# Batch 5 joins the batches whose q is transposed by DMA; the transposing transfers are issued by SyncE, in a new order of work

## The chip, the cores and the metric

The kernel runs on one core of one Trainium2 chip. The metric is device time in microseconds (us) of one execution, inputs and output in HBM. Five engines of the core work side by side, each through its own list of instructions in order: TensorE (PE; its weight loads are shown as PEld), VectorE (DVE), ScalarE (ACT), GpSimd (POOL) and SyncE (SP). Engines wait for each other by semaphores. DMA transfers are issued here by POOL (loads that turn float32 into bfloat16), by SP and by ACT.

## The reference

A linear attention without softmax, normed per head, followed by a gated feed-forward with a convolution over three positions:

```python
batch, n_heads, seq, head_dim = (8, 8, 576, 64)
kv = np.einsum('bhsd,bhse->bhde', k, v)
out = np.einsum('bhsd,bhde->bhse', q, kv)
rms = np.sqrt(np.mean(out * out, axis=-1, keepdims=True) + 1e-06)
attn = (out / rms * g_norm).astype(np.float32)
x = attn.transpose(0, 2, 1, 3).reshape(8, 576, 512)
h = np.maximum(x @ w_in, 0.0)                    # 512 -> 1024
conv_out = sum of conv_w[k] * (h shifted by k - 1 along the sequence), k = 0, 1, 2
gate = 1.0 / (1.0 + np.exp(-conv_out))
result = (h * gate) @ w_out                      # 1024 -> 512
```

The last four lines are shortened; all else is as in the reference.

## The kernel before

**Tiles.** A batch's q, k and v lie in SBUF as 96 partitions by 8 heads by 6 rows of 64 (sequence position = 6 x partition + row), in bfloat16. Two heads make one tile `t` of 128 rows (4 tiles a batch); two tiles make a half `u`. Two batches make a pair `p`.

**Steps**, by their names in the order; the numbers after a name are batch (or pair, or convolution stage), then tile:
- `Lq`, `Lk`, `Lv` (L296), `Li` (w_in), `Lo` (w_out): loads, issued by POOL. q, k and v have two buffers each, so a load waits until the batch two before has been read.
- `kv` (L353): 48 products of 64x64 that sum k^T v over a batch's rows into one PSUM bank; `kvc` copies them into `kvbd`, 128x128 blocks with two heads on the diagonal, zero elsewhere.
- `qt` (L375): TensorE transposes half a batch's q, 24 products; `qc` copies the result to SBUF (`qT`) on DVE or ACT.
- `ot` (L414, L415): q times kvbd for one tile, 64 and then 512 columns at full 128x128.
- For the batches in `QD` (6 and 7) another way: `dq` (L420) issues a transposing DMA of half a batch's q from SBUF to SBUF, which leaves the rows in a different arrangement; `kvn` copies the sums of k^T v without zeros; `kx` (L432), twice, issues a small DMA that puts the other half's rows into `kvx`; `oq` (L442) computes a tile as four 64x64 products of 288 columns at four positions of the array. `sq` and `oc` read that product in the other arrangement.
- `sq` squares the product on ACT, `oc` copies it to SBUF as float32, `ss` sums squares per head on TensorE, `ln` and `sl` make the inverse root, `sp` (L577) spreads it over the rows, `mu` (L584) multiplies into x. Batches 0 and 1 have a shorter way (`on`, `nl`, `mu0`).
- `hm` (L595): x times w_in for one batch and one of 8 blocks `f` of 128 features, 8 products of 288 columns; `re` (L601 on ACT, L603 on DVE) is the relu.
- `ta`, `aa`, `ab` (DVE) make the convolution, `sg` (L656, ACT) the sigmoid, `mg` (DVE) multiplies.
- `om` (L672): h times w_out for 128 rows, 8 products of 512 columns (pairs 0 and 3 in two halves of 4); `ea` copies to one of 8 row buffers; `st` (L683) stores it, issued by SP.
- `unread.n`: n products whose result nobody reads.

**Order.** `ORDER` is one list, written out. The loop at L685 emits one step after the other, and at the end every instruction is tied to its predecessor on its own engine (L695 to L703). So each engine works through its own instructions in the list's order; between engines only data, PSUM banks (the numbers after `@`) and buffers make anyone wait. A step further down the list can start earlier than one above it if it is on another engine. `:1` switches a copy or relu to the other one of ACT and DVE.

What an engine issues counts in this: a `dq` in ACT's list holds back ACT's later steps until it is issued, and a wait in SP's list holds back all later `kx`, `st` and `dq` on SP. In the old order SP issues two loads at the start and then nothing until `kx.6.0`.

Of the kernel before, what the change touches and what calls it, by code (L numbers as in the profile page):

```python
# [73 lines left out]
unread.3@7 ot.1.3@6 sq.1.3@6 ot.1.2@0 aa.0.3 unread.2@2 on.1.3@4 sq.1.2@7 on.1.2@2 ab.0.3 nl.1.3@6 hm.0.3@4 nl.1.2@7
hm.0.2@2 mu0.1.3 mu0.1.2 sg.0.1 sg.0.0 re.0.2:1 Lk.2.0@0 sg.0.6 re.0.3 hm.1.3@0 hm.1.0@6 hm.0.5@2 mg.0.0 hm.0.4@4
ta.0.2@0 sg.0.7 re.1.3 ta.0.3 re.0.5 re.0.4 mg.0.3 aa.0.1 re.1.0 kv.2.0.4@0 hm.1.2@4 kvc.2.0.4.0@0 ab.0.1 ta.0.4@1
sg.0.2 Lq.2.0@0 sg.0.3 ta.0.5 hm.1.7@6 hm.1.6@2 aa.0.2 re.1.2 qt.2.0@4 mg.0.1 ab.0.2 re.1.7 Lq.3.0@1 kvc.2.0.4.1
re.1.6 qt.2.1@0 sg.0.5 sg.0.4 qc.2.0@4 ot.2.1@4 Lv.3.0@1 Lk.3.0@1 sq.2.1@0 ot.2.0@2 sq.2.0@1 qc.2.1@0 ta.1.2@0
hm.1.4@6 ta.1.3 mg.0.2 oc.2.0@0 hm.1.1@0 aa.1.1 re.1.4 oc.2.1 ta.1.0@1 ab.1.1 re.1.1 ot.2.2@2 qt.3.1@6 qt.3.0@4
qc.3.1@1 qc.3.0@2 sq.2.2@2 sg.1.2 sg.1.3 hm.1.5@0 oc.2.2:1@1 ta.1.1 ot.2.3@6 mg.1.1 Lo.0 re.1.5 sq.2.3@3 kv.3.0.4@4  # L80
kvc.3.0.4.0@1 al.x2@1 ss.2@5 al.x1@0 kvc.3.0.4.1 oc.2.3 unread.1@0 ot.3.0@2 sq.3.0@4 oc.3.0@2 Lo.1 ot.3.1@0 aa.1.0
ot.3.2@6 Lq.4.0@0 sq.3.2@5 om.0.3.0@4 ta.1.4@0 ab.1.0 ta.1.5 sq.3.1@6 ln.8@0 om.0.0.0@2 om.0.2.0@3 oc.3.2:1@3 aa.1.2
ot.3.3@6 sq.3.3@7 om.0.0.4 om.0.3.4 om.0.2.4 oc.3.1 oc.3.3 ab.1.2 ea.0.3@0 Lk.4.0@0 sl.8@0 sp.2.0@6,0 ss.3@5
om.0.1.0@4 mu.2.0.0 mu.2.0.1 Lv.4.0@0 ea.0.2@1 ea.0.0@2 ln.1@0 sp.2.1@2,6 mu.2.1.1 mu.2.1.0 om.0.1.4 sg.1.5 sl.1@0
qt.4.1@0 qt.4.0@6 qc.4.1:1@3 ea.0.1@3 hm.2.6@2 hm.2.2@0 qc.4.0@4 re.2.6 sp.3.1@2,6 sg.1.1 re.2.2 kv.4.0.4@4 mu.3.1.0
mu.3.1.1 sg.1.0 mg.1.0 hm.2.4@0 Lv.5.0@1 Lk.5.0@1 kvc.4.0.4.0@0 sp.3.0@6,2 mu.3.0.0 mu.3.0.1 kvc.4.0.4.1 hm.2.5@4
ta.1.6@1 re.2.4 sg.1.4 re.2.5 Lq.5.0@1 ot.4.2@6 hm.2.7@0 ot.4.0@4 sq.4.2@0 Lv.6.0@0 Lq.6.0@0 ta.1.7 oc.4.2@1
Lk.7.0@0 mg.1.2 aa.1.3 sq.4.0@1 hm.3.4@2 re.2.7 re.3.4 hm.3.6@6 ot.4.3@0 ab.1.3 oc.4.0@0 re.3.6 hm.3.5@2 ta.2.4@0
# [25 lines left out]
om.3.7.4 om.2.6.0@4 om.3.5.0@6 om.3.8.0@1 ea.3.3@0 ea.3.0@5 ea.3.7@1 st.3.3 st.1.5 om.3.5.4 om.3.8.4 ea.2.6@0 st.2.5
om.3.2.0@0 om.3.4.0@7 ea.3.5@4 st.2.2 ea.3.8@6 st.3.7 st.3.5 st.3.8 st.3.0 om.3.2.4 om.3.4.4 om.3.6.0@1 om.3.1.0@6
om.3.6.4 ea.3.2@7 st.3.2 st.2.6 om.3.1.4 ea.3.4@1 ea.3.6@4 st.3.4 st.2.1 st.2.0 st.3.6 ea.3.1@6 st.3.1
"""


# [1 line left out]
def kernel(  # L121
# [295 lines left out]
    @op  # L417
    def dq(b, u):
        s = T["qx", b, u] = ring("qT", [P, 2, S], BF16, name="qT").rearrange("p t (h n) -> p (t h n)", n=PS)
        nc.scalar.dma_start_transpose(  # L420
            out=s.rearrange("p (c n) -> p c n", n=PS),
            in_=qkv["q", b][:, 4 * u:4 * u + 4, :].rearrange("p h d -> p (h d)"))

# [310 lines left out]
```

## Time and profile before

| | us |
|---|---|
| median of 3 executions | 182.5 (181.41 to 183.57) |
| the profiled execution, whole | 182.38 |
| its span, first to last instruction | 180.6 |
| PE busy | 170.6 (94% of the span) |
| ACT busy | 149.0 (83%) |
| DVE busy | 140.5 (78%) |
| POOL busy | 31.0 (17%) |
| transposing transfers (4), issue to landing | 4.9 to 5.6, median 5.2 |
| copies into kvx (4), issue to landing | 2.5 to 4.3, median 4.0 |

The granted clock of TensorE is 1.0 throughout. The chain of work that ended last is on PE for 57% of the span and on ACT for 19%. The costliest groups are `hm` on PE (512 products, 67.7 us), `om` on PE (288 products, 65.7 us), the sigmoid (41.8 us) and the relu (39.7 us) on ACT.

In a line of the timeline the first number is the start in us from the span's start, the second how long it took, then engine, source line, operation, output and input tile, and how many instructions were merged. `ACTq` and `SPq` are the sequencers of ACT and SP while they issue a DMA. A bracket gives how long the engine sat idle before the instruction and what, by the profile, it waited for. The ends of products on PE are modelled, so their bars overlap by a little.

### The profile page before, as it was taken

What the parts mean: (1) busy time and instruction counts of PE and PEld (TensorE: products, weight loads), DVE (VectorE), ACT (ScalarE), POOL (GpSimd) and SP (SyncE); (2) the same over time, 40 slices, a digit from 0 to 9 for tenths busy, and PEclk for the clock granted to TensorE, in tenths of its full rate; (3) what the DMA queues carried; (4) which work ended last, traced back from release to release, by engine and by line L of the source; (5) the groups of instructions that cost most, each with busy time, mean ns of one, the idle gap of its engine ahead of it and who ended that gap; (6) DMA issues with size and microseconds to landing.
All of it is one profiled execution on the core that took longest, in us unless ns stands there. A gap on an engine that the chain in (4) does not pass through costs nothing.

```text
span 180.6 us, 4135 instructions
## 1 busy us (share of the span) xinstructions
PE 170.6 (94%) x1700; PEld 100.9 (56%) x1700; DVE 140.5 (78%) x237; ACT 149.0 (83%) x233; POOL 31.0 (17%) x54
## 2 busy tenths in 40 slices
...
GB/s 150 187 183 193 200 201 203 203 205 208 203 204 203 203 204 203 205 207 165 243 237 195 5 0 104 12 4 58 0 331 21 0 0 81 210 3 205 147 279 241
DMA packets 32474, 27.57 MB, mean 153 GB/s; under 512 B 6064, under 2 KB 27848, under 8 KB 32456
## 3 DMA queue, kind: packets, MB, share of 16 engines
...
q8 instruction: 13, 0.21, 0.5%
...
## 4 chain that ended last, share of the span: by engine, by line
PE 57%; ACT 19%; DVE 8%; DMA 5%; POOL 5%; issue 4%; ACTq 1%; POOLq 0%; DVEq 0%
PE bank L672 31%; PE bank L595 21%; ACT h L601 6%; DMA v_sb<-in_v_dram 5%; ACT taps L656 4%; ACT sq L469 3%; ACT L208 2%; ACT o L336 2%; DVE xT L584 2%; POOL q_sb L236 1%; DVE qT L338 1%; PE bank L375 1%; DVE taps L637 1%; DVE taps L638 1%; POOL k_sb L236 1%
## 5 line engine op out<-in xcount | busy, mean ns | idle before, releaser
L595 PE MATMUL bank<-xT,w_in_sb 128*128 128x288 bf16 x512 | 67.7, 286 | 1.1 <-ACT h L601 0.8
L672 PE MATMUL bank<-w_out_sb,h 128*128 128x512 bf16 x288 | 65.7, 379 | 0.0
L595 PEld LDWEIGHTS <-w_in_sb 128*128 128x128 bf16 x512 | 49.1, 98 | 17.0 <-issue 2.5
L672 PEld LDWEIGHTS <-h 128*128 128x128 bf16 x288 | 27.4, 98 | 31.5 <-issue 0.7
L656 ACT ACTIVATE taps<-taps,cwn 128x1152 bf16<-128x1152 bf16 (+1 forms) x40 | 41.8, 1083 | 2.5 <-DVE taps L650 1.6
L601 ACT ACTIVATE h<-bank 128x576 bf16<-128x576 f32 x63 | 39.7, 670 | 4.3 <-DVE taps L638 1.6
L336 ACT ACTIVATE row<-bank 128x512 f32<-128x512 f32 x35 | 20.6, 617 | 11.6 <-PE bank L672 11.1
L662 DVE TENSOR_TENSOR h<-h,taps 128x2304 bf16<-128x2304 bf16 (+1 forms) x20 | 22.2, 1112 | 3.4 <-ACT taps L656 3.4
L644 DVE TENSOR_TENSOR taps<-taps 128x2304 bf16<-128x2304 bf16 (+1 forms) x20 | 22.3, 1115 | 0.3
L650 DVE TENSOR_TENSOR taps<-taps,h 128x2304 bf16<-128x2304 bf16 (+1 forms) x20 | 22.2, 1112 | 0.2
L637 DVE TENSOR_SCALAR taps<-h,cwn 128x1152 bf16<-128x1152 bf16 (+1 forms) x40 | 18.4, 460 | 5.0 <-ACT h L601 5.0
L584 DVE SCALAR_TENSOR_TENSOR xT<-o,cw,bank 128x576 bf16<-128x576 f32 x24 | 18.6, 809 | 2.2 <-PE bank L577 2.1
L469 ACT ACTIVATE sq<-bank 128x576 bf16<-128x576 f32 x28 | 18.4, 694 | 1.0 <-PE bank L415 1.0
L638 DVE TENSOR_SCALAR taps<-h,cwn 128x1152 bf16<-128x1152 bf16 (+1 forms) x40 | 18.0, 451 | 0.0
L336 ACT ACTIVATE o<-bank 128x576 f32<-128x576 f32 x22 | 15.1, 717 | 0.0
L411 PE MATMUL bank<-fill 128*128 128x512 bf16 x35 | 10.8, 435 | 2.5 <-DVE fill L223 1.5
...
L353 PEld LDWEIGHTS <-k_sb 96*64 96x64 bf16 x384 | 7.4, 112 | 3.7 <-issue 3.3
L296 POOL DMA_DIRECT2D v_sb<-in_v_dram x8 | 6.1, 768 | 18.1 <-PE bank L353 17.0
L353 PE MATMUL bank<-v_sb,k_sb 96*64 96x64 bf16 x384 | 8.3, 197 | 0.7 <-DMA v_sb<-in_v_dram 0.3
L375 PEld LDWEIGHTS <-q_sb 96*64 96x64 bf16 x288 | 6.9, 110 | 3.5 <-DMA q_sb<-in_q_dram 1.9
L375 PE MATMUL bank<-ident,q_sb 96*64 96x96 bf16 x288 | 8.1, 208 | 0.7 <-DMA q_sb<-in_q_dram 0.6
...
## 6 DMA issues: line engine op xcount, KB each, us to landing
...
```

Source lines behind the costliest of these rows:

```text
L336: nc.scalar.activation(to, fr, AX.Copy)
L469: nc.scalar.activation(in_order(b, s), product(b, t), AX.Square)
L584: nc.vector.scalar_tensor_tensor(x_tile(b)[:, 2 * u:2 * u + 2, n], T["o32", b, u][:, :, n], g_sb, T["sp", b, e][u][:, :, :HS], op0=AL.mult ...
L595: nc.tensor.matmul(ps[:, e, :HS], w_in_sb[:, t, f * P:(f + 1) * P], x[:, t, e * HS:(e + 1) * HS], start=(t == 0), stop=(t == NT - 1))
L601: nc.scalar.activation(to, fr, AX.Relu)
L637: nc.vector.tensor_scalar_mul(tap[:, 0, f % 2, :n, 8:8 + S], h[:, f], cwn[:, 0, f:f + 1])
L638: nc.vector.tensor_scalar_mul(tap[:, 1, f % 2, :n, :S], h[:, f], cwn[:, 2, f:f + 1])
L644: nc.vector.tensor_add(tap[:, 1, :, :n, :S], tap[:, 0, :, :n, 7:7 + S], tap[:, 1, :, :n, 1:1 + S])
L650: nc.vector.tensor_add(y, y, h[:, 2 * j:2 * j + 2])
L656: nc.scalar.activation(y, y, AX.Sigmoid, scale=cwn[:, 1, f:f + 1])
L662: nc.vector.tensor_mul(h, h, T["tap", c, j][:, 1, :, :n, :S])
L672: nc.tensor.matmul(T["om", p, m], h[:, f, m * P:(m + 1) * P], w_out_sb[:, f, :], start=(f == 0), stop=(f == NF - 1))
```

## The change

Batch 5 is added to `QD`. Its two `qt`, two `qc`, two `kvc` and four `ot` go; two `dq`, one `kvn`, two `kx` and four `oq` come. Every `dq`, those of batches 6 and 7 too, is issued by SP instead of ACT. All steps are put into a new order with new banks and some copies on the other engine. SP's list now runs `dq.5.0 kx.5.0 dq.5.1 kx.5.1 st.0.2 dq.7.0 kx.7.0 kx.6.0 kx.7.1 st.0.3 st.0.1 dq.7.1 dq.6.0 st.0.0 dq.6.1 kx.6.1` and then stores. Loads of batch 5 are now issued as q, v, k (before: v, k, q); those of batches 6 and 7 as k6, v7, k7, q7, v6, q6 (before: v6, q6, k7, k6, v7, q7).

```diff
 SPLIT = (0, 3)
-QD = (6, 7)
+QD = (5, 6, 7)
...
-kv.0.3.1@4,5 kvc.0.3.1.0 on.0.2@2 kvc.0.3.1.1:1 ot.0.3@4 nl.0.2@2 al.h1@0 sqh.0.3.0@3 unread.3@7 onh.0.3.0@2
-qt.1.0@6 sqh.0.3.1 nlh.0.3.0@3 qc.1.0:1@2 onh.0.3.1 unread.3@6 kv.1.0.2@6 mu0.0.2 muh.0.3.0 nlh.0.3.1 Lk.1.2 Lq.1.2
-Lv.1.2 kvc.1.0.2.0@1 kvc.1.0.2.1 muh.0.3.1 al.h0@1 Li.1 Li.2 Lv.2.0@0 unread.3@0 ot.1.1@6 hm.0.0@4 pl sq.1.1@4
...
-sq.4.3@2 ot.4.1@6 kv.5.0.4@4 re.3.5 Lk.6.0@1 oc.4.3 ta.2.5 sq.4.1@3 qt.5.1@2 qt.5.0@0 kvc.5.0.4.0:1@1 qc.5.1@0
-oc.4.1 Lv.7.0@1 ss.4@5 sg.1.6 sg.1.7 hm.3.7@6 kvc.5.0.4.1:1 ot.5.2@2 om.0.4.0@4 qc.5.0@2 ot.5.0@0 re.3.7 sq.5.2@4
-aa.2.2 oc.5.2@2 hm.3.2@6 mg.1.3 Lq.7.0@1 sq.5.0@5 oc.5.0@3 ot.5.3@2 ab.2.2 sq.5.3@6 re.3.2 oc.5.3 sg.2.5 sg.2.4
-om.0.4.4 om.0.5.0@0 ot.5.1@6 om.0.6.0@1 hm.2.0@2 ta.2.6@1 om.0.5.4 sq.5.1@7 om.0.6.4 ta.2.7 ea.0.4:1@4 oc.5.1
-hm.2.3@6 ss.5 ea.0.5@5 aa.2.3 mg.2.2 ab.2.3 ln.2@0 kv.6.0.4@0 hm.3.3@4 ta.2.2@0 ea.0.6@6 dq.6.0@1 re.2.3 re.2.0
-sl.2@0 re.3.3 kvn.6:1 om.0.7.0@1 sp.4.0@6,2 om.0.7.4 mu.4.0.0 mu.4.0.1 sp.5.0@4,6 sg.2.6 kv.7.0.4@0 mu.5.0.0
-mu.5.0.1 hm.2.1@2 sp.5.1@4,6 kx.6.0 st.0.2 ta.2.3 kvn.7 dq.7.0@3 st.0.3 mu.5.1.0 aa.2.1 re.2.1 mu.5.1.1 om.0.8.0@0
-st.0.4 hm.3.1@2 kx.6.1 st.0.1 st.0.5 om.0.8.4 sg.2.7 ea.0.7@7 ab.2.1 hm.3.0@4 dq.6.1@4 re.3.1 sp.4.1@2,6 ea.0.8@1
-al.h2@1 re.3.0 dq.7.1@0 hm.5.3@0 mu.4.1.0 hm.5.1@4 sg.2.3 mg.2.3 re.5.3 mu.4.1.1 ta.2.0@1 ta.2.1 hm.5.2@2 hm.4.1@0
-oq.6.0@6 re.5.1 aa.2.0 ab.2.0 hm.5.7@4 sg.2.2 st.0.8 kx.7.0 al.x3@0 re.4.1 sq.6.0@0 re.5.2 hm.4.2@0 mg.2.1 hm.5.0@2
...
-kx.7.1 re.4.4 oc.6.2@2 oc.6.1 om.1.7.0@6 ea.1.7@0 oq.6.3@2 oq.7.0@4 sq.6.3@3 sq.7.0@4 oq.7.2@0 oc.6.3 oc.7.0@0
...
+unread.3@3 onh.0.3.0@6 nlh.0.3.0@3 onh.0.3.1 qt.1.0@2 nlh.0.3.1 qc.1.0:1@2 mu0.0.2 muh.0.3.0 Lq.1.2 muh.0.3.1 Lv.1.2
+hm.0.6@6 hm.0.7@4 Lk.1.2 re.0.6 re.0.7 unread.3@0 kv.1.0.2@4 kvc.1.0.2.0@1 kvc.1.0.2.1 unread.3@0 ot.1.1@4 ot.1.0@6
+sq.1.1@4 unread.2@0 on.1.1@2 sq.1.0@5 nl.1.1@4 hm.0.0@0 ta.0.6@0 Li.2 re.0.0 ta.0.7 qt.1.1@2 aa.0.3 qc.1.1:1@3
+mu0.1.1 on.1.0@4 Li.1 hm.0.1@0 nl.1.0@5 ta.0.0@1 ab.0.3 kv.1.2.2@2 kvc.1.2.2.0 kvc.1.2.2.1 re.0.1 unread.3@3
+ot.1.2@2 mu0.1.0 ta.0.1 sq.1.2@6 aa.0.0 ot.1.3@6 unread.2@4 on.1.2@0 ab.0.0 sq.1.3@7 nl.1.2@6 Lk.2.0@0 on.1.3@4 pl
...
+kvc.3.0.4.1:1 qt.3.1@2 qc.3.0@1 qc.3.1@2 oc.2.3 Lo.1 Lv.4.0@0 sg.1.3 sg.1.2 Lk.4.0@0 Lq.4.0@0 unread.1@4 ot.3.0@0
+aa.1.2 ot.3.1@6 ot.3.3@2 unread.1@4 om.0.0.0@4 sq.3.0@4 oc.3.0@2 mg.1.1 om.0.1.0@0 sq.3.1@5 Lq.5.0@1 oc.3.1 ot.3.2@6
...
+hm.3.5@6 ot.4.2@2 sq.4.0@0 oc.4.0@0 re.3.5 sq.4.2@1 dq.5.0@0 Lk.6.0@0 hm.3.1@4 hm.2.6@0 ot.4.1@6 mg.1.0 ab.1.3
+ta.2.4@1 re.3.1 oc.4.2@1 sq.4.1@2 ta.2.5 hm.3.3@4 kv.5.0.4@2 oc.4.1 re.2.6:1 aa.2.2 kvn.5:1 sg.1.6 ot.4.3@6 hm.3.6@0
+re.3.3 hm.3.7@4 kx.5.0 sg.1.7 ab.2.2 sq.4.3@3 re.3.6 oc.4.3 hm.2.3@2 hm.3.0@6 hm.2.2@0 mg.1.3 re.3.7 dq.5.1@1
+ta.2.6@0 hm.3.2@4 sg.2.4 re.2.3 kx.5.1 re.3.0 ta.2.7 st.0.2 aa.2.3 re.2.2:1 sg.2.5 oq.5.1@6 oq.5.0@2 re.3.2 sq.5.0@4
+sq.5.1@5 ab.2.3 om.0.8.0@0 hm.2.1@4 oc.5.0@2 re.2.1 Lv.7.0@0 Lk.7.0@1 oc.5.1 om.0.8.4 oq.5.2@2 oq.5.3@4 mg.2.2
+ta.2.2@1 ss.4@1 sq.5.3@6 ta.2.3 sq.5.2@7 om.0.6.0@6 om.0.4.0@7 ss.5 om.0.4.4 ln.2@0 aa.2.1 oc.5.2@3 om.0.6.4
+ea.0.4@4 sl.2@0 ea.0.8@5 kv.7.0.4@7 ea.0.6@6 sp.4.1@0,2 oc.5.3 kvn.7 ab.2.1 mu.4.1.1 mu.4.1.0 om.0.7.0@6 Lq.7.0@0
+Lv.6.0@1 om.0.5.0@7 sp.4.0@2,4 sg.2.2 dq.7.0@2 kx.7.0 Lq.6.0@1 mu.4.0.0 mu.4.0.1 om.0.5.4 sp.5.0@0,2 mu.5.0.0
+mu.5.0.1 om.0.7.4 ea.0.5@7 sg.2.3 kv.6.0.4@7 sp.5.1@0,4 ea.0.7@2 al.x3@0 al.h2@0 hm.4.0@2 kvn.6 mg.2.1 mu.5.1.0
+mu.5.1.1 hm.4.3@6 ta.2.0@1 hm.4.2@0 ta.2.1 sg.2.6 hm.4.4@4 sg.2.7 re.4.3 re.4.0 kx.6.0 kx.7.1 mg.2.3 aa.2.0 re.4.2
+oq.7.0@2 oq.7.1@6 re.4.4 st.0.3 st.0.1 dq.7.1@3 hm.5.2@0 hm.5.3@4 sq.7.0@0 oc.7.0@0 ab.2.0 re.5.2 sq.7.1@1 oc.7.1
+re.5.3 hm.5.0@2 hm.5.5@0 re.5.0 ta.3.2@0 hm.5.4@4 hm.4.1@2 sg.2.0 re.5.5 hm.5.1@0 dq.6.0@4 st.0.0 hm.5.6@6 ta.3.3
+aa.3.1 dq.6.1@0 ab.3.1 sg.2.1 re.4.1 re.5.4 re.5.1 hm.4.6@2 kx.6.1 hm.4.5@0 re.5.6 mg.2.0 ta.3.0@1 om.1.6.0@6 sg.3.2
...
     @op
     def dq(b, u):
         s = T["qx", b, u] = ring("qT", [P, 2, S], BF16, name="qT").rearrange("p t (h n) -> p (t h n)", n=PS)
-        nc.scalar.dma_start_transpose(
+        nc.sync.dma_start_transpose(
             out=s.rearrange("p (c n) -> p c n", n=PS),
             in_=qkv["q", b][:, 4 * u:4 * u + 4, :].rearrange("p h d -> p (h d)"))
```

More of the change, by code (lines that the diff above doesn't have):

```diff
@@ L74 @@
[L74 to L88, printed above, removed]
@@ L114 @@
[L114 to L116 removed]
+pre@0,0,0 unread.10@0 qt0.0.0@0 qc0.0.0:1@0 pn ps pi Lq.1.0@1 ca.k.0 ca.v.0 kv.0.0.1@1 ct@2 qt0.0.1@3 qc0.0.1:1
+kvc.0.0.1.0:1@0 pg kvc.0.0.1.1:1 ot.0.0@0 sq.0.0@0 Li.3 pc al.h0@0 al.x0@0 unread.3@4 kv.0.1.1@3 al.x2@1 Lv.1.0@1
@@ new lines @@
+kvc.0.1.1.0:1 on.0.0@4 nl.0.0@0 Lk.1.0@1 kvc.0.1.1.1:1 al.h1@1 unread.1@6 qt0.0.2@3 ot.0.1@6 sq.0.1@1 unread.4@2
+kv.0.2.1@2 qc0.0.2:1@1 on.0.1@4 mu0.0.0 kvc.0.2.1.0 nl.0.1@1 kvc.0.2.1.1:1 mu0.0.1 qt0.0.3@3 ot.0.2@0 unread.3@2
+kv.0.3.1@2,4 Li.0 sq.0.2@2 qc0.0.3:1 kvc.0.3.1.1 on.0.2@6 kvc.0.3.1.0:1 nl.0.2@2 ot.0.3@4 sqh.0.3.0@3 sqh.0.3.1
+unread.3@3 onh.0.3.0@6 nlh.0.3.0@3 onh.0.3.1 qt.1.0@2 nlh.0.3.1 qc.1.0:1@2 mu0.0.2 muh.0.3.0 Lq.1.2 muh.0.3.1 Lv.1.2
+hm.0.6@6 hm.0.7@4 Lk.1.2 re.0.6 re.0.7 unread.3@0 kv.1.0.2@4 kvc.1.0.2.0@1 kvc.1.0.2.1 unread.3@0 ot.1.1@4 ot.1.0@6
@@ new lines @@
+re.1.4 ta.0.5 kv.2.0.4@0 re.1.6 qt.2.0@6 ab.0.1 qt.2.1@2 aa.0.2 re.1.2 Lv.3.0@1 Lk.3.0@1 sg.0.2 kvc.2.0.4.0:1@0
+sg.0.3 hm.1.3@4 ab.0.2 kvc.2.0.4.1 qc.2.0@4 qc.2.1@0 ot.2.1@6 ot.2.0@0 hm.1.5@2 sg.0.5 sg.0.4 mg.0.1 Lq.3.0@1 re.1.3
+sq.2.0@0 sq.2.1@1 mg.0.2 re.1.5:1 hm.1.7@4 ta.1.2@1 ta.1.3 oc.2.0@0 oc.2.1 ta.1.4@0 ot.2.2@2 re.1.7 hm.1.1@0
+ot.2.3@6 sq.2.2@2 re.1.1 sq.2.3@3 aa.1.1 ta.1.5 Lo.0 ab.1.1 kv.3.0.4@4 kvc.3.0.4.0@1 ss.2@5 oc.2.2@1 qt.3.0@0
+kvc.3.0.4.1:1 qt.3.1@2 qc.3.0@1 qc.3.1@2 oc.2.3 Lo.1 Lv.4.0@0 sg.1.3 sg.1.2 Lk.4.0@0 Lq.4.0@0 unread.1@4 ot.3.0@0
@@ new lines @@
+aa.1.2 ot.3.1@6 ot.3.3@2 unread.1@4 om.0.0.0@4 sq.3.0@4 oc.3.0@2 mg.1.1 om.0.1.0@0 sq.3.1@5 Lq.5.0@1 oc.3.1 ot.3.2@6
+ab.1.2 om.0.2.0@1 ln.8@0 om.0.1.4 sq.3.2@6 sq.3.3@7 oc.3.2@3 om.0.2.4 om.0.0.4 ta.1.0@1 ta.1.1 aa.1.0 sl.8@0 oc.3.3
+ea.0.1@0 sp.2.0@6,2 ss.3@5 al.x1@0 ab.1.0 ea.0.0@1 mu.2.0.1 ln.1@0 mu.2.0.0 om.0.3.0@0 sg.1.5 sp.2.1@4,2 mu.2.1.0
+mu.2.1.1 sl.1@0 om.0.3.4 Lv.5.0@1 sg.1.4 ea.0.2@2 hm.2.7@4 mg.1.2 ta.1.6@0 hm.2.0@2 re.2.7 re.2.0 hm.2.4@6
+sp.3.1@2,4 ea.0.3@3 Lk.5.0@1 kv.4.0.4@1 mu.3.1.0 mu.3.1.1 re.2.4 hm.2.5@6 sg.1.1 sp.3.0@2,4 kvc.4.0.4.0@0 ta.1.7
@@ new lines @@
+ea.1.6@3 st.1.6 ta.3.5 hm.4.7@2 sq.6.2@3 sq.6.0@4 om.1.3.0@6 oc.6.0@2 oc.6.2@3 re.4.7 ea.1.1@0 oq.6.1@0 oq.7.3@2
+aa.3.2 sq.6.1@5 oq.6.3@4 om.1.7.0@7 st.0.5 st.0.7 sq.6.3@6 oc.6.1 sq.7.3@7 ss.6@0 ss.7 om.1.0.0@1 ln.3@0 oc.6.3
+ab.3.2 ea.1.7@1 st.1.1 oc.7.3 om.1.5.0@0 ea.1.0@3 sg.3.4 sl.3@0 sp.7.1@2,4 mu.7.1.1 sg.3.5 om.1.4.0@1 st.1.0
+ea.1.3@7 mu.7.1.0 ea.1.5@2 sp.7.0@2,4 om.1.2.0@7 mu.7.0.0 mu.7.0.1 sp.6.1@4,2 mg.3.2 om.1.8.0@6 mu.6.1.1 st.1.3
+mu.6.1.0 al.h3@1 ta.3.6@0 sg.3.0 hm.5.7@2 ea.1.2@0 ea.1.4@3 ea.1.8@7 sp.6.0@6,4 re.5.7 mu.6.0.0 ta.3.7 mu.6.0.1
```

34 lines of the change are left out of this document (14 added, 20 removed).

## The prediction

> **What bounds the kernel now.** I began with the busy table by stretches. The stretches were cut where the chain of waits changes character: loads and short stages up to 29.4 us, then four stretches up to 177 us, where the last product of w_out ends.
>
> ```profile
> core 0: us, PE busy (x) PEld busy (x) DVE busy (x) ACT busy (x) POOL busy (x), PEclk, DMA share, GB/s
> 29.40:50.00 20.60, 19.81 (x314) 14.73 (x314) 19.44 (x39) 20.48 (x36) 4.72 (x7) 1.00 1.30 204
> 50.00:82.40 32.40, 32.37 (x401) 19.90 (x399) 30.00 (x50) 32.29 (x53) 5.03 (x7) 1.00 1.31 204
> 82.40:98.30 15.90, 15.04 (x200) 9.60 (x196) 15.01 (x25) 12.85 (x19) 0.00 (x0) 1.00 1.14 224
> 98.30:127.00 28.70, 28.69 (x214) 15.63 (x214) 24.79 (x33) 28.64 (x45) 0.00 (x0) 1.00 0.08 29
> 127.00:177.00 50.00, 49.94 (x296) 28.05 (x292) 33.69 (x41) 35.41 (x50) 0.00 (x0) 1.00 0.33 122
> ```
>
> The second number of a line is the stretch, the third PE's busy time. From 29.4 us to 177 us TensorE is idle for 147.6 - 145.85 = 1.75 us only, so a microsecond of TensorE work removed there, or of wait added, counts nearly in full. ACT and DVE are almost as full up to 82 us, so they may take over. The stretch 82.4 to 98.3 is the exception: ACT is busy for 12.85 of 15.9 us. Bars of products overlap and hide short gaps, so I checked it by pace. Eight `hm` groups of 8 products (128 products took 15.79 us in the chain of waits, so 0.99 us a group), four half groups of `om` (144 products in 31.09 us, 0.86 us a half), two `kv` (0.88 us) and four `sp` (0.21 us) make 14.0 us of work in 15.85 us. About 1.9 us is lost, 0.83 us of it in one visible piece. The timeline says why:
>
> ```profile
> 87.99 2.14 ACTq L420 DMA_TRANSPOSE qT<-q_sb  x1
> 88.22 0.36 ACT L336 ACTIVATE kvn<-bank 128x256 bf16<-128x256 f32 x1
> ...
> 89.10 0.52 DVE L638 TENSOR_SCALAR taps<-h,cwn 128x1152 bf16<-128x1152 bf16 x1
> ...
> 90.23 0.65 ACT L601 ACTIVATE h<-bank 128x576 bf16<-128x576 f32 x1 [1.65 <-DVE taps L638]
> ...
> 90.93 1.14 PE L595 MATMUL bank<-xT,w_in_sb 128*128 128x288 bf16 x8 [0.83 <-ACT h L601]
> ```
>
> ACT's sequencer is in the transposing transfer until 90.13 us. The relu behind it starts at 90.23 us, although what the profile names (DVE, L638) ended at 89.62 us; TensorE waits for that relu.
>
> **What leaves TensorE.** The transposes of batch 5 (`qt.5.1`, `qt.5.0`) and the products of one batch before and after, from the timeline of PE:
>
> ```profile
> 57.85 1.21 PE L375 MATMUL bank<-ident,q_sb 96*64 96x96 bf16 x48
> 58.99 2.13 PE L595 MATMUL bank<-xT,w_in_sb 128*128 128x288 bf16 x16
> ...
> 109.89 0.31 PE L442 MATMUL bank<-qT,kvn 64*64 64x288 bf16 x1
> ...
> 110.59 3.63 PE L672 MATMUL bank<-w_out_sb,h 128*128 128x512 bf16 x16
> ```
>
> A batch's 48 transposes hold PE from 57.85 to 58.99: -1.14 us. Three `oq` lie between 109.89 and 110.59, 0.23 us each; all eight in this profile took 1.75 us, 0.22 each. An `ot` takes about 0.245 us (64.48 to 64.73 with its neighbours): four of them save 0.10 us. The page TensorEngine Tiling (Array Packing) of the Trainium skill, section Key Properties, has the four tiles work independently and the array drain at each change of mode. If the four ran wholly side by side, an `oq` would cost a quarter of its four 288-column products (0.49 us at 0.123 us each), 0.12 us, and this term would be -0.5 us; the trace shows 0.22 us with the changes of mode, and that is used. The new order also has 39 filling products where the old had 35. At 0.21 us that is 0.86 us, but three of the four lie before 29.4 us, where PE waits for loads (the last k, v of batch 1 land at the same place in the stream of loads), and one lies where PE waits for the copies of batch 3's q. I take +0.1 (0 to 0.86).
>
> **What leaves DVE and ACT.** DVE loses two qT copies (0.75 us each), and two kvbd copies become one kvn copy (0.42 us less). Some copies change sides: by the new order's choices DVE is about 2 us lighter, ACT about 0.8 us heavier. Neither is paid directly, since TensorE ends the waits; they loosen or tighten what is below.
>
> **The issues moved to SP.** Four transfers held ACT's sequencer for 1.40, 2.14, 2.41 and 1.33 us. Much of it was covered by work already queued on ACT. What reached PE is at most the 0.83 us above; DVE explains it up to 89.62 us, so the transfer is good for the last 0.5 us. I take -0.5 (0 to -0.83). The page DMA: Bandwidth & Descriptors of the Trainium skill, section Issuing engines are not separate DMA queues, says that another issuing engine saves only issue time, usually small beside the transfer. By that rule the term is 0 and the sum 0.5 us higher; the trace has 1.3 to 2.4 us of issue beside 5.0 to 5.6 us to landing, which is not small.
>
> **The wait added.** In the old order batch 6's first `oq` came about 13 us of PE work after `kv.6`. In the new order SP issues `dq.5.0`, `kx.5.0`, `dq.5.1`, `kx.5.1`, and PE has only `ot.4.3` and six `hm` between `kv.5` and `oq.5.1`: 0.25 + 6 x 0.99 = 6.2 us. `oq.5.1` needs both halves of kvx, and the second, `kx.5.1`, stands behind a transposing transfer that it does not need. The rows for that chain, from what the trace has on the tile kvn (the SP line is the issue; the last line counts from issue to landing):
>
> ```profile
> L432 SPq DMA_DIRECT2D kvx<-kvn x4: 472/506/747, 85.7 to 94.8; - x4
> ...
> L338 DVE CAST kvn<-bank x1: 415/415/415, 85.2 to 85.2; 128x256 bf16<-128x256 f32 x1
> ...
> DMA to landing us min/median/max: 2.5/4.0/4.3
> ```
>
> The 2.5 us is the copy issued alone; 4.3 us is one issued 0.9 us after a transposing transfer on the other queue. The chain from the end of `kv.5`: wait for DVE 0.65 (as long as the copy waited after batch 5's `kv` here; 0 to 1.36, one addition ahead of it), kvn copy 0.41, issue of `kx.5.0` 0.54 (0.47 to 0.75), issue of `dq.5.1` 1.8 (1.33 to 2.41), landing of `kx.5.1` 4.3. That is 7.7 us against 6.2 us of cover: +1.5 us on PE. Low end: 0 + 0.41 + 0.47 + 1.33 + 2.5 = 4.7, hidden. High end: no row shows a copy behind a transposing transfer on one queue; with the slowest transposing landing, 5.6, it is 1.36 + 0.41 + 0.75 + 2.41 + 5.6 = 10.5, +4.3 us. I take 4.3 for the landing as the only row with both in flight.
>
> The same happens once more: `kx.7.1` is queued behind `kx.6.0`, which waits for `kvn.6`, copied by ACT after `kv.6`. Chain: 0.3 (ACT's queue; to 0.65) + 0.36 + 0.54 + 2.5 (to 4.3) = 3.7 us (to 5.9); PE has `sp.5.1` and four `hm`, 4.2 us. I take +0.2 (0 to 1.7). Stores queued behind SP's waits lose nothing before the tail: eight row buffers, and the old first store went out at 86 us.
>
> **Loads.** Up to 84 us loads fill the queue at 204 GB/s, 576 KB in 2.9 us. `dq.5` now falls into that stream, and k of batch 5 is loaded last of the three instead of second. That is one load plus the share taken by a transposing transfer later, some 70 us, just when PE arrives at `kv.5` (69.5 us before). +0.1 (0 to 1.5).
>
> **Given back.** A PE that waits at `oq.5.1` lets ACT and DVE run ahead, so part of the other 1.1 us lost in 82 to 98 us should go: -0.5 (0 to -1.1).
>
> **Sum.** -1.14 - 0.10 + 0.1 - 0.5 + 1.5 + 0.2 + 0.1 - 0.5 = -0.3 us. The profiled execution took 182.38 us, 180.6 us of it the span; the median of three is 182.5, so either base will do: 182.0 us.
>
> **Rivals.** Faster: the copies land inside their cover (low ends), and a freed ACT closes the whole loss between 82 and 98 us: -1.14 - 0.10 - 1.9 = -3.1, 179.3 us. For it: adding up durations by kind along both orders, ACT has up to 4 us less work behind it at equal PE work in the new one between 45 and 100 us. Against it: the chain on SP, whose cover is half the old one.
> Slower: the copies of kvx stick on SP. It starts at `kx.5.1`, at its high end +4.3, and repeats at `kx.7.1`, +1.7; with -1.24 and -0.5 that is +4.3, 186.7 us. It decides from the point where the two waits exceed 3.5 us together, that is when `kvx` of batch 5 lands over about 9.5 us after `kv.5`. For it: one queue for both kinds, untried before, under full loads. Against: all transposing landings were 5.0 to 5.6 us, the first under loads too.
> The order itself loses: all else is moved as well, and banks turn around within 1.3 us of PE work in as many places as before (28 pairs before, 30 after), each one a possible wait behind ACT or DVE; +2.5, 184.9 us.
> The move does not free ACT: the relu waited for DVE or for something not shown; +0.5, 182.5 us.
>
> **Chances.** As summed 0.35, its own range 180.7 to 184.1; move without effect 0.07; faster rival, whole or in part, 0.27; SP rival 0.21; order rival 0.10. A difference under 1% (1.8 us) cannot be told from none here. So faster 0.27, within 1% 0.42, slower 0.31. The range 179.4 to 185.6 takes in the faster rival's price nearly and the slower ones up to halfway past the order's.
>
> **What would show it.** No transposes of batch 5 on PE and no transposing transfer on ACT's queue: ACT's idle time between 82 and 98 us below 2 us. The first `oq` after `kv.5` idle for 1 to 2 us for kvx, with `kx.5.1` landing 7 to 8 us after `kv.5`. PE idle in 29.4 to 177 us near 2.5 us. The forecast is wrong if PE shows no wait at `oq.5.1` (then faster), if that wait is over 3 us, or if PE idles over 2 us where none of these names apply.

## The result, and the profile after

| | before | after |
|---|---|---|
| median, us | 182.33 (181.41 to 183.57, 4 runs) | 189.26 (188.55 to 189.52, 4 runs) |
| the profiled execution, us | 182.38 | 189.52 |
| its span, us | 180.6 | 187.8 |
| PE busy, us (share) | 170.6 (94%) | 171.7 (91%) |
| granted clock of TensorE, mean | 1.00 | 0.982 |
| transposing transfers, issue to landing, us | 4.9 to 5.6 | 3.7 to 12.0, median 10.5 |
| copies into kvx, issue to landing, us | 2.5 to 4.3 | 2.1 to 9.4, median 2.6 |

The ratio is 1.0365, with an interval of 1.0319 to 1.0412: the change costs 7 us. The rows of TensorE and of its clock on the page of the kernel after, 40 slices of 4.7 us each:

```profile
PE   6999999999999999409999999999999999999990
...
PEclk9999999999999999975999999999999999999999
```

TensorE has one hole, in two slices around 80 us, and in the second of them and in the one behind it the granted clock falls. The busy table by stretches of the kernel after puts numbers on it (columns as in the table of before: PE, PEld, DVE, ACT, POOL, then the clock):

```profile
50.00:70.00 20.00, 19.79 (x228) 12.37 (x230) 19.51 (x38) 19.51 (x34) 1.72 (x3) 1.00 1.31 201
70.00:82.40 12.40, 7.32 (x99) 5.64 (x99) 12.18 (x17) 8.32 (x13) 2.29 (x3) 1.00 1.31 188
82.40:98.30 15.90, 13.57 (x127) 6.14 (x131) 5.43 (x9) 10.72 (x17) 0.77 (x1) 0.79 0.92 116
98.30:127.00 28.70, 28.55 (x269) 17.86 (x270) 26.94 (x35) 28.62 (x45) 0.00 (x0) 1.00 0.38 100
```

Up to 70 us and from 98.3 us on PE is as full as before. Between them 5.1 us are idle in one stretch and 2.3 us in the next, which runs at a mean clock of 0.79. The timeline of the kernel after, PE and SP together, names the place:

```profile
62.46 2.35 SPq L420 DMA_TRANSPOSE qT<-q_sb  x1
...
69.96 0.95 PE L353 MATMUL bank<-v_sb,k_sb 96*64 96x64 bf16 x48
...
71.09 6.04 PE L595 MATMUL bank<-xT,w_in_sb 128*128 128x288 bf16 x48
71.47 0.54 SPq L432 DMA_DIRECT2D kvx<-kvn  x1
72.12 2.82 SPq L420 DMA_TRANSPOSE qT<-q_sb  x1
74.99 0.59 SPq L432 DMA_DIRECT2D kvx<-kvn  x1
...
77.07 0.31 PE L442 MATMUL bank<-qT,kvn 64*64 64x288 bf16 x1
84.40 0.45 PE L442 MATMUL bank<-qT,kvx 64*64 64x288 bf16 x2 [7.03 <-DMA kvx<-kvn]
...
86.71 2.13 PE L595 MATMUL bank<-xT,w_in_sb 128*128 128x288 bf16 x8
```

The first product of `oq.5.1` (it reads kvn) runs at 77.07 us; the next needs kvx and waits 7.03 us. Behind the wait an `hm` group takes 2.13 us, where one alone took 1.14 before: the clock records are at half from 82.46 to 89.29 us. The chain of work that ended last, in the kernel after, runs through this copy:

```profile
74.43 0.51 SPq L420
74.94 0.04 issue
74.99 9.37 DMA kvx<-kvn
84.36 0.04 issue
84.40 0.69 PE bank L442 x7
```

`kx.5.1`, 32 KB, needs 9.37 us from its issue to its landing; it stands on SP right behind `dq.5.1`. `kx.5.0`, 0.65 us before `dq.5.1`, took 5.6 us.

What the DMA engines did meanwhile is in the DMA view of the kernel after (a queue's packets, MB, share of 16 engines' time): the first line is from 52 to 61 us, with loads alone (q0), the other two from 67 to 72 us, with `dq.5.0` under way (q1):

```profile
q0 software_dynamic: 2432, 1.83, 131.5%
...
q0 software_dynamic: 936, 0.70, 90.5%
q1 hardware_dynamic: 935, 0.24, 37.6%
```

Loads alone move 270 packets per us (of 752 bytes on average). With the transposing transfer beside them it is 187 and 187: one packet of 256 bytes for one of 750. So half a batch of q, 288 KB, which is 1,152 such packets, needs 6.2 us for its packets alone, and the loads fall from 203 to 140 GB/s. The turns are a good half of the 11.6 us that `dq.5.0` took; its first packet moved only 4.0 us after its issue.

In the kernel before, the first transposing transfer was issued beside loads too, but late in their stream. The first line is its issue (timeline); the other two are the DMA view from 84 to 86 us, where q10 is the queue of ACT:

```profile
82.56 1.40 ACTq L420 DMA_TRANSPOSE qT<-q_sb  x1
...
q10 hardware_dynamic: 461, 0.12, 125.5%
q0 software_dynamic: 126, 0.09, 29.5%
```

Its packets moved from 83.8 us on, as the loads ran out, and it landed after 5.3 us. The other three, from 87.99 us on, met no loads. The two of batch 5 in the kernel after are issued at 62 and 72 us into the full stream, and land after 11.6 and 12.0 us.

The balance of the two profiled spans: +7.2 us = +7.0 (the wait) + about 2.4 (the half clock, sized below) - about 2.2 (all the rest of the change).

### The profile page after: what moved, and what is told of

Same layout as the page of the kernel before. It is cut to its first block, busy times and chain, and to the rows that moved or that the text cites. A ratio compares the mean times of both kernels' runs of the same rounds, so it can differ in the third digit from the quotient of the medians.

```text
span 187.8 us, 4053 instructions
## 1 busy us (share of the span) xinstructions
PE 171.7 (91%) x1646; PEld 101.0 (54%) x1664; DVE 139.6 (74%) x234; ACT 149.9 (80%) x233; POOL 30.6 (16%) x54
## 4 chain that ended last, share of the span: by engine, by line
PE 63%; ACT 25%; DMA 5%; issue 3%; DVE 2%; SPq 0%; DVEq 0%; ACTq 0%
PE bank L672 30%; PE bank L595 18%; ACT h L601 7%; ACT taps L656 7%; ACT sq L469 5%; DMA kvx<-kvn 5%; PE bank L411 5%; ACT o L336 3%; PE bank L375 2%; PE bank L353 2%; PE bank L577 1%; PE bank L549 1%; ACT row L336 1%; PE bank L415 1%; PE bank L414 1%
## 5 line engine op out<-in xcount | busy, mean ns | idle before, releaser
L595 PEld LDWEIGHTS <-w_in_sb 128*128 128x128 bf16 x512 | 49.9, 99 | 16.5 <-issue 2.6
L601 ACT ACTIVATE h<-bank 128x576 bf16<-128x576 f32 x60 | 38.0, 680 | 4.4 <-PE bank L595 4.1
L336 ACT ACTIVATE row<-bank 128x512 f32<-128x512 f32 x36 | 21.1, 606 | 13.1 <-PE bank L672 12.0
L336 ACT ACTIVATE o<-bank 128x576 f32<-128x576 f32 x24 | 16.0, 698 | 0.0
L411 PE MATMUL bank<-fill 128*128 128x512 bf16 x37 | 12.3, 448 | 1.6 <-DVE fill L223 1.5
L565 DVE CAST hi<-rs 128x288 bf16<-128x288 f32 x4 | 1.2, 309 | 12.0 <-ACT rs L558 11.9
L296 POOL DMA_DIRECT2D k_sb<-in_k_dram x8 | 6.0, 750 | 20.2 <-PE bank L353 19.5
L442 PE MATMUL bank<-qT,kvx 64*64 64x288 bf16 x24 | 2.7, 320 | 7.0 <-DMA kvx<-kvn 7.0
L536 DVE SCALAR_TENSOR_TENSOR xT<-bank,cw,root 128x576 bf16<-128x576 f32 x7 | 5.6, 815 | 4.6 <-ACT root L518 4.6
```

The costliest lines, as they stand in the source:

```text
L336: nc.scalar.activation(to, fr, AX.Copy)
L411: nc.tensor.matmul(ps[:, :512], fill[:, :P], fill, start=True, stop=True)
L595: nc.tensor.matmul(ps[:, e, :HS], w_in_sb[:, t, f * P:(f + 1) * P], x[:, t, e * HS:(e + 1) * HS], start=(t == 0), stop=(t == NT - 1))
L601: nc.scalar.activation(to, fr, AX.Relu)
```

## The experiments

The theory formed from the two traces: the copies of kvx of batch 5 stick on SP's queue behind a transposing transfer that the loads slow down. Rivals: any place behind a transposing transfer is as late, whatever the queue; the copies are only issued too late; the new order of everything else loses by itself; the move of the issues loses. Each expectation spells out those that its run tells apart. Each run has the kernel before beside it on its chip, at medians of 182.5 us in the first eight, 182.7 in the two after them and 183.3 in the last.

**Both copies of batch 5 on another queue.** `kx.5.0` and `kx.5.1` issued by ACT:

```diff
-        nc.sync.dma_start(out=T["kvx", b][i * D:(i + 1) * D], ...)
+        (nc.scalar if b == 5 else nc.sync).dma_start(out=T["kvx", b][i * D:(i + 1) * D], ...)
```

> The changed kernel, but the two copies into kvx of batch 5 are issued by ACT instead of SP. Theory 1 (one queue): in the changed kernel kx.5.1 landed 9.4 us after its issue because it stood in SP's queue behind the transposing transfer dq.5.1, whose packets take turns with those of the loads. Then both copies now land within 6 us of their issue (kx.5.0 took 5.6 there, with nothing ahead of it), PE waits under 1.5 us at oq.5.1 instead of 7.0, the clock stays at 1.0, and since dq.5.1 no longer stands behind a copy that waits for kvn, it is issued near 65 us and lands before oq.5.2 needs it: 181 to 183 us. Theory 2 (loads): under full loads any small copy takes 9 us, whatever its queue: PE waits some 7 us again, 188 to 190 us. Theory 3 (issue): the hardware that makes descriptors is shared and held by the transposing transfers; the copies are late by the same 2 to 4 us or more on ACT too, and ACT stalls while it issues: 185 to 189 us.

186.6 us (185.35 to 187.31), ratio 1.0208 (1.015 to 1.0266). The timeline of this kernel (ACTq is ACT's sequencer):

```profile
62.15 8.20 SPq L420 DMA_TRANSPOSE qT<-q_sb  x2
...
74.27 0.47 ACTq L432 DMA_DIRECT2D kvx<-kvn  x1
...
82.61 0.45 PE L443 MATMUL bank<-qT,kvx 64*64 64x288 bf16 x2 [4.76 <-DMA kvx<-kvn]
```

Only 2.3 us of the wait go. The edit moved a second thing: with no `kx` between them SP issued both transposing transfers in one go, so both stood ahead of the copies. `kx.5.0` landed 9.9 us after its issue; its first packet moved 5.7 us after it, as the transposing packets ended. A queue of its own is not enough when two transposing transfers are ahead; why is open. The next two runs change less.

**Only the second copy on another queue**, all else in its order:

```diff
+        (nc.scalar if (b, i) == (5, 1) else nc.sync).dma_start(
```

> The changed kernel with one copy alone, kx.5.1, issued by ACT; kx.5.0, dq.5.0 and dq.5.1 stay on SP in their order, so what was issued ahead of the copy is as in the changed kernel and only its queue differs. Theory 1 (one queue): on ACT's own queue the copy does not stand behind dq.5.1; it is issued near 74 us and lands within 6 us, PE's wait at oq.5.1 falls from 7.0 to 2 to 3 us; 183 to 185 us. Theory 3 (transfers issued by SP and ACT are served in the order of issue whatever their queue, and a transposing transfer under loads takes 6 to 8 us of that service): the copy lands near 83 to 84 us again, after dq.5.1's last packet, the wait is 5.5 to 7.5 us; 187.5 to 189.5 us. The run with both copies on ACT spoke for theory 3 (first packet of the copy 5.7 us after its issue, when the transposing packets ended), but there dq.5.1 had also moved forward.

184.85 us (184.42 to 185.29), ratio 1.0138 (1.0082 to 1.0193). From the timeline of this kernel:

```profile
72.17 2.48 SPq L420 DMA_TRANSPOSE qT<-q_sb  x1
74.30 0.54 ACTq L432 DMA_DIRECT2D kvx<-kvn  x1
...
80.39 0.31 PE L443 MATMUL bank<-qT,kvx 64*64 64x288 bf16 x2 [2.96 <-DMA kvx<-kvn]
```

Issued at the same time relative to `dq.5.1`, but by ACT, the copy lands after 6.1 us instead of 9.4, and its packets lie among those of `dq.5.1`. So 3.3 us of its landing were the place behind `dq.5.1` on one queue, under the loads; the other 6 are not. The wait of 2.96 us still brings the half clock (80.9 to 84.3 us).

**The copies ahead of the second transposing transfer**, all on SP:

```diff
-... hm.3.7@4 kx.5.0 sg.1.7 ... re.3.7 dq.5.1@1 ... re.2.3 kx.5.1 re.3.0
+... hm.3.7@4 kx.5.0 kx.5.1 dq.5.1@1 sg.1.7 ... re.3.7 ... re.2.3 re.3.0
```

> The changed kernel with SP's order dq.5.0, kx.5.0, kx.5.1, dq.5.1 instead of dq.5.0, kx.5.0, dq.5.1, kx.5.1. Theory 1: kx.5.1 lands 5 to 6 us after an issue near 72 us, the wait at oq.5.1 shrinks from 7.0 to under 1.5 us; dq.5.1, issued half a us later than before, lands some 12 us after its issue as it did (84 to 85 us), and the wait moves to oq.5.2, 3 us of PE work later: 2 to 5 us there; 183 to 187 us. Theory 2: kx.5.1 still takes 9 us, the wait at oq.5.1 is 4 us or more. Theory 3: as theory 1 for kx.5.1, since only dq.5.0 lies ahead of it.

185.22 us (184.91 to 185.53), ratio 1.014 (1.0075 to 1.0205). From PE's timeline in this kernel:

```profile
77.52 0.31 PE L442 MATMUL bank<-qT,kvx 64*64 64x288 bf16 x2 [0.57 <-DMA kvx<-kvn]
...
83.95 0.31 PE L442 MATMUL bank<-qT,kvn 64*64 64x288 bf16 x1 [3.18 <-DMA qT<-q_sb]
```

The wait for kvx falls from 7.03 to 0.57 us, and a new one stands at `oq.5.2`: for `dq.5.1` itself, which lands too late under the loads. It brings the half clock too (84.2 to 87.6 us). The order on SP decides which of the two transfers is late, not that one is.

**The same transfers without competing loads.** q, k and v of batches 6 and 7 are not loaded; these batches compute with batches 4 and 5 again, so a quarter of the output is left out:

```diff
     def load(x, b, t0):
+        if b in (6, 7):
+            slots.pop(0)
+            qkv[x, b] = qkv[x, b - 2]
+            return
```

> The changed kernel without the loads of q, k and v of batches 6 and 7: those two batches read the rows of batches 4 and 5 instead, all other work stays. Loads then end near 68 us instead of 92. If the alternation of packets with loads made dq.5.1 slow (12.0 us to landing), it now lands in 5 to 6 us and kx.5.1 behind it in 4 to 6 us, and the wait at oq.5.1 falls from 7.0 to under 2 us although the queue and its order are the same: 180 to 184 us. If standing in one queue behind a transposing transfer costs that much by itself, the wait stays at 5 to 7 us: 187 to 189 us.

180.55 us (one run), clock 1.0. From the timeline of this kernel:

```profile
72.34 1.31 SPq L424 DMA_TRANSPOSE qT<-q_sb  x1
73.70 0.83 SPq L436 DMA_DIRECT2D kvx<-kvn  x1
...
77.29 0.31 PE L446 MATMUL bank<-qT,kvn 64*64 64x288 bf16 x1
77.29 0.31 PE L446 MATMUL bank<-qT,kvx 64*64 64x288 bf16 x2
```

Same queue, same order, and `kx.5.1` still right behind `dq.5.1`: the product with kvx follows with no wait. The issue of `dq.5.1` takes 1.31 us instead of 2.82, and it lands after 3.4 us; `kx.5.1` lands 2.2 us after its issue, so without loads the place behind a transposing transfer costs next to nothing. Its counterpart is the kernel before with the same edit:

> The kernel before without the loads of q, k, v of batches 6 and 7; these batches compute with batches 4 and 5 again, so the output of a quarter of the batches is left out. It is the counterpart of the same edit in the kernel after, which took 180.55 us. Theory 1: the kernel before has no wait on the loads or their traffic between 50 and 85 us, so it keeps 181.5 to 182.5 us, and the batch 5 change without competing loads is worth -1 to -2 us, near the -1.24 us of the prediction's products and copies. Rival (fewer loads make any order faster): 180.5 us or less, and the change gains nothing even without the loads.

182.96 us (182.32 to 184.29), ratio 1.0009 (0.9977 to 1.0041). Fewer loads give the old order nothing. So the change without loads beside its transfers is worth about 180.55 - 182.96 = -2.4 us, and with them +6.9. The -2.4 is rough: one side is a single run, and the two ran on different chips; against the kernel before on its own chip (182.48) the single run is 1.9 us faster.

**The half clock by itself.** 32 products whose result nobody reads, ahead of `oq.5.1`, so that PE is not idle in the wait:

```diff
-... sg.2.5 oq.5.1@6
+... sg.2.5 unread.32@6 oq.5.1@6
```

> The changed kernel with 32 products that nobody reads (about 6.9 us at 0.21 us each) put on PE ahead of oq.5.1, into a bank that is free, so that PE works through its wait of 7.0 us. The wait itself stays. In the changed kernel the granted clock fell to half from about 82.5 to 89.3 us, so that 8 products of hm took 1.92 us instead of 0.98: if the slowed products are a part of the loss, the clock now stays at 1.0 and the time falls by 2 to 3 us to 186.3 to 187.3 us; if the lower clock only covers time that PE would have waited anyway, it stays at 188.5 to 189.5 us.

186.91 us (186.71 to 187.32), ratio 1.024 (1.0189 to 1.0291). PE in this kernel:

```profile
76.77 7.07 PE L411 MATMUL bank<-fill 128*128 128x512 bf16 x32
83.77 0.31 PE L442 MATMUL bank<-qT,kvn 64*64 64x288 bf16 x1
...
85.22 1.14 PE L595 MATMUL bank<-xT,w_in_sb 128*128 128x288 bf16 x8
```

PE reaches kvx 7 us late as before, but the `hm` behind takes 1.14 us again. 189.26 - 186.91 = 2.35 us of the loss are the half clock. It fits the records: behind the wait 4.9 us of work ran at half clock, which is 2.4 us lost.

**The move of the issues, in the new order**: all `dq` back on ACT.

```diff
-        nc.sync.dma_start_transpose(
+        nc.scalar.dma_start_transpose(
```

> The changed kernel and its order with all transposing transfers issued by ACT again: the move to SP undone, batch 5 and the new order kept. Theory 3: the copies on SP's queue still come behind dq.5.1 if that was issued first, and dq.5.1 itself lands late, so PE waits 3 to 7 us at oq.5.1 or oq.5.2, and ACT loses 2 to 5 us more to issues of 1.3 to 2.8 us each under loads: 188 to 192 us. Theory 1: with separate queues the wait at oq.5.1 falls under 2.5 us, a wait of 2 to 4 us at oq.5.2 for dq.5.1 remains: 184 to 187 us.

189.22 us (187.55 to 189.95), ratio 1.0364 (1.0313 to 1.0416), as the kernel after. PE in this kernel:

```profile
80.81 0.28 PE L442 MATMUL bank<-qT,kvn 64*64 64x288 bf16 x1 [1.90 <-ACT h L601]
...
87.36 0.31 PE L442 MATMUL bank<-qT,kvn 64*64 64x288 bf16 x1 [2.86 <-DMA qT<-q_sb]
```

The waits change their names: the relu behind ACT's issues (`dq.5.1` held ACT for 3.29 us from 75.03), then `dq.5.1`'s landing. kvx is no longer late: the two copies, issued on SP ahead of `dq.5.1`, land after 4.9 and 6.1 us.

**The move of the issues, in the old order**: the kernel before, every `dq` on SP.

```diff
-        nc.scalar.dma_start_transpose(
+        nc.sync.dma_start_transpose(
```

> The kernel before with one edit: its four transposing transfers (batches 6 and 7) are issued by SP instead of ACT, the order stays. The prediction's term for this is -0.5 us (0 to -0.83): ACT's sequencer is free between 88.0 and 90.1 us and the relu behind it starts up to 0.6 us earlier. If that is right, 181.5 to 182.2 us beside 182.4. If the issue on ACT held nothing up, 182.4. If SP's queue now makes kx or stores late, 183 us or more; against that, loads have nearly ended by the first of them (82.6 us).

181.38 us (180.9 to 181.79, 12 runs) against 182.51, ratio 0.993 (0.9904 to 0.9957). The timeline of this kernel:

```profile
74.15 1.84 SPq L420 DMA_TRANSPOSE qT<-q_sb  x1
...
89.07 1.04 PE L672 MATMUL bank<-w_out_sb,h 128*128 128x512 bf16 x4
89.94 1.14 PE L595 MATMUL bank<-xT,w_in_sb 128*128 128x288 bf16 x8
```

TensorE's gap behind ACT's relu (0.83 us before, at 90 us) is gone. `dq.6.0`, no longer held by ACT's list, is issued at 74.15 us, under the loads, and lands after 11.8 us, as batch 5's do; here the product that reads it comes at 97 us, and nothing waits. This part of the change alone is worth -1.1 us (-0.8 to -1.8 by the interval of the ratio).

**A mend by hand**: copies first, and `oq.5.2`, `oq.5.3` put behind `om.0.6` and `om.0.4`, with `kv.7` and two `om` moved up.

```diff
-oq.5.2@2 oq.5.3@4 mg.2.2 ... om.0.6.0@6 om.0.4.0@7 ... om.0.4.4 ... om.0.6.4
+mg.2.2 ... om.0.6.0@6 om.0.6.4 om.0.4.0@7 om.0.4.4 ... oq.5.2@2 oq.5.3@4
```

> The version with kx.5.1 ahead of dq.5.1 and, beyond that, oq.5.2 and oq.5.3 put behind 3.5 us more of PE work (both halves of om.0.6 and om.0.4), with kv.7, om.0.7 and om.0.5 moved forward to stand between oq.5.3, ss.5 and sp.4.1. If the waits of PE for batch 5's transfers and the slow clock after them are the whole loss, both waits fall under 0.5 us each, the clock stays at 1.0 and the time is 180.5 to 182.5 us, at or under that of the kernel before. If transposing under loads costs more than these waits (slower loads, a later dq.6), it stays at 183.5 us or more.

186.84 us (186.33 to 189.58), ratio 1.0237 (1.0194 to 1.0281): not the 180.5 to 182.5 us expected. The trace is of the slowest of the four executions, 189.58 us. In it PE waits 0.91 us for kvx and not for `dq.5.1`, but four waits of 0.4 to 1.7 us come at the `sp` steps between 92.9 and 96.9 us, whose norm chain now starts later, and the clock records are at half from 96.8 to 103.7 us. By this trace the cover for a 12 us transfer was taken from another chain; no run shows that apart.

**The new order without batch 5's transfers.** Batch 5 back on TensorE at the same places (`qt`, `qc`, `kvc`, `ot`); the issues of batches 6 and 7 stay on SP:

```diff
-QD = (5, 6, 7)
+QD = (6, 7)
...
-... re.2.3 kx.5.1 re.3.0 ta.2.7 st.0.2 aa.2.3 re.2.2:1 sg.2.5 oq.5.1@6 oq.5.0@2 ... om.0.8.0@0
+... re.2.3 qt.5.0@2 qc.5.0@0 re.3.0 qt.5.1@6 qc.5.1@1 ta.2.7 st.0.2 aa.2.3 re.2.2:1 sg.2.5 om.0.8.0@0 ot.5.1@2 ot.5.0@6
```

> The kernel after, in its own new order and with SP issuing the transposing transfers of batches 6 and 7, but batch 5 is put back on TensorE: transposes, copies into kvbd and ordinary products (ot) at the places of the oq, and no dq and kx of batch 5. Theory 1 (the whole loss is the wait of batch 5's copies and its half clock, 7.0 + 2.35 us of the kernel after; the new order by itself is neutral): both go, the work of batch 5 comes back (+1.14 + 0.10 us), the issue time of the other transfers stays off ACT as in the kernel before with SP issuing (-1.1): 181 to 182.5 us, granted clock 1.0, PE busy in 70 to 98 us nearly all the time. Rival (the new order loses as such, hidden so far under the waits): 184 us or more, with new waits on PE spread over the span. Third reading (the new order saves by itself): under 180.5 us.

187.42 us (186.46 to 188.75), ratio 1.0232 (1.0178 to 1.0285), clock 0.982: the time is the rival's, but the waits are not spread over the span. The timeline of this kernel:

```profile
79.26 1.42 DVE L338 COPY qT<-bank 128x1152 bf16<-128x1152 bf16 x2 [3.08 <-ACT taps L656]
...
83.66 0.58 PE L672 MATMUL bank<-w_out_sb,h 128*128 128x512 bf16 x1 [4.00 <-DVE h L603]
```

It was my placement: the two copies stood in DVE's list ahead of work that was ready, and held it for 3.1 us until PE had transposed; the relu `re.2.2` behind them came at 82.86 instead of 76.72 us, and the next bank waited for that. The copies were then put behind that relu:

```diff
-re.2.3 qt.5.0@2 qc.5.0@0 re.3.0 qt.5.1@6 qc.5.1@1 ta.2.7 st.0.2 aa.2.3 re.2.2:1 sg.2.5
+re.2.3 qt.5.0@2 re.3.0 qt.5.1@6 ta.2.7 st.0.2 aa.2.3 re.2.2:1 qc.5.0@0 qc.5.1@1 sg.2.5
```

> As the kernel with batch 5 back on TensorE, but the two copies of batch 5's qT stand behind the last relu of DVE instead of ahead of it (in the former placement DVE sat idle for 3.1 us before them, that relu came at 82.86 us instead of 76.7, and PE waited 4.0 us for it with the half clock behind). Theory 1 (new order neutral, the loss belongs to batch 5's copies): the 4.0 us and most of the half clock go, PE has no wait over 1 us between 70 and 98 us, 181 to 182.5 us. Rival (the new order loses as such): 184 us or more, with the idle time of PE in other places than before oq/ot of batch 5.

181.82 us (181.28 to 184.78) against 183.26, ratio 0.9911 (0.9877 to 0.9945). PE in this kernel:

```profile
80.10 1.21 PE L375 MATMUL bank<-ident,q_sb 96*64 96x96 bf16 x48
81.24 1.04 PE L672 MATMUL bank<-w_out_sb,h 128*128 128x512 bf16 x4
...
85.70 0.19 PE L414 MATMUL bank<-qT,kvbd 128*128 128x64 bf16 x1 [1.07 <-ACT o L336]
```

The trace is of the slowest of the seven executions, 184.78 us; in it the transposes hold PE for 1.14 us, between 70 and 98 us one wait of 1.07 us is left, and the clock stays. The ratio agrees, within the intervals, with that of the old order with the issues on SP (0.993): the new order itself neither saves nor costs anything that can be told here, and the whole loss belongs to batch 5's transfers. These two are the fastest versions of the study that compute the whole output, 0.7 and 0.9% ahead of the kernel before.

## Why the prediction was wrong

Forecast 182.0 us, range 179.4 to 185.6; measured 189.26. The mechanism is the one of its rival for slower, the copies of kvx that stick on SP, which it priced at 186.7 us with a chance of 0.21.

**The step that failed is the wait added**, +1.5 us (0 to 4.3) in the sum and 7.0 on the chip. By its own chain from the end of `kv.5`, 70.84 us:

| | forecast, us | measured, us |
|---|---|---|
| wait for DVE and kvn copy | 1.06 | 0.60 |
| issue of `kx.5.0` | 0.54 | 0.54 |
| issue of `dq.5.1` | 1.8 (1.33 to 2.41) | 2.82 |
| landing of `kx.5.1` | 4.3 (2.5 to 5.6) | 9.37 |
| gaps between them | - | 0.19 |
| sum | 7.7 | 13.5 |
| cover on PE | 6.2 | 6.5 |

The landing is most of it. Its bounds came from transfers of the kernel before whose packets moved when the loads were ending or over. The argument against the rival, that the first transposing landing had been under loads too, holds for its issue alone (82.56 us): from 84 to 86 us it moved 461 packets beside 126 of the loads, where `dq.5.0` met them one for one. In the old order without the loads of batches 6 and 7 the same transfer landed after 3.4 us instead of 5.3.

The rows for the copy were misread as well. The one of 2.5 us, called "issued alone", was issued at 85.66 us, while that transposing transfer was under way (to 87.86 us); so the 4.3 us was not the only row with both in flight, and neither had loads beside it to speak of. Without loads the same transfers in the same order cost no wait (77.29 us, no bracket), and `kx.5.1` landed after 2.2 us. Of the 9.4 us under loads some 3.3 were the place behind `dq.5.1` on SP's queue (6.1 us from ACT's queue); the rest is the copy itself under those loads.

**A term that was missing: the clock.** No line has a price for a slower clock behind a long wait; it cost 2.35 us. The Trainium skill, page TensorE: Matmul & The Clock Gate, section What's actually happening, gives half rate after an idle window of about 3.4 us. The runs agree in kind, but shorter waits sufficed: after 1.07 and 1.90 us the clock stayed, after 2.86, 2.96 and 3.18 us it fell to half. It stayed there for 3.4 us behind these three and behind a wait of 4.76 us, and for 6.8 us behind waits of 4.00 and 7.03 us, so its length does not simply follow the wait's. In the mend by hand a row of waits of 1.7 us at most brought 6.8 us of it too.

**The rest of the sum held as a total.** Without the wait its terms add up to -1.14 - 0.10 + 0.1 - 0.5 + 0.2 + 0.1 - 0.5 = -1.84 us; the balance of the spans leaves about -2.2, and the pair without loads gives about -2.4. That does not show each term, and part of it may be luck: the new order with the issues on SP and batch 5 on TensorE is already 0.9% faster than the kernel before, and with batch 5's transfers but without loads the one run is 1.1% faster than it. What those transfers gain when nothing waits for them can't be told from this. One by one:
- Transposes and products, -1.24: the prediction's row at 57.85 us is of batch 4's transposes; batch 5's stand behind `kv.5`, from 70.30 to 71.45 us, 1.15 us, which changes nothing. The two last `oq` of batch 5 took 0.37 us together (89.91 to 90.28), 0.19 each, between the 0.22 used and the 0.12 of full overlap. In the last experiment the transposes alone hold PE for 1.14 us.
- Issues moved to SP, -0.5 (0 to -0.83): -1.1 in the old order, beyond the range, though the interval (-0.8 to -1.8) reaches it. The 0.83 us gap is gone; where the rest came from is not shown. The rule of the Trainium skill that was weighed there (DMA: Bandwidth & Descriptors, Issuing engines are not separate DMA queues) is that another issuing engine saves only the issue time, usually small beside the transfer. Here that saving was worth more than the term, and the measurement decides. Its other half, that transfers interleave whichever engine issued them, agrees with 936 packets against 935; but the issuer did matter for the copy behind a transposing transfer (6.1 against 9.4 us). In the new order with batch 5 the move brings nothing (189.22 against 189.26).
- `kx.7.1`, +0.2: no wait for it; PE is idle for 0.15 us in the whole stretch from 98.3 to 127 us.
- Loads, +0.1: `kv.5` starts at 69.96 us with no wait. The loads did lose a third of their rate to the transposing transfers, but nobody on PE waited for one.
- Filling products, +0.1, and what DVE and ACT gain: not tried alone. Given back, -0.5: covered by the stop, can't be told.

**The other rivals.** The faster one had the copies inside their cover: only without loads. The order that loses by itself (+2.5): refuted by the last experiment. The move that does not free ACT (+0.5): refuted in the old order.

**What would show it**: the list had the case, "that wait is over 3 us". PE's idle time from 29.4 to 177 us, forecast near 2.5, is 8.7 us. ACT's idle time between 82 and 98 us (5.2 us) follows from the stop and tells nothing of the issues.

**Open.** Why a copy on ACT's queue behind two transposing transfers moves no packet for 5.7 us, why the first packet of `dq.5.0` moves 4.0 us after its issue when that of the transfer issued at 82.56 us in the kernel before moved after 1.2 us, and what sets the time that the issue itself takes (2.82 us under loads and 8.20 for two together, against 1.31 without; but also 1.40 at 82.56 us beside loads, and 2.41 without any). That loads and transposing transfers take turns packet by packet is read from the counts; other packet sizes weren't tried.
